# When the held output chunks run, and which buffers the last batch's loads and outputs use

## The chip, the cores and the metric

The kernel runs on one core of one Trainium2 chip. A core has a matmul engine (TensorE, PE in the profile), which writes into PSUM banks; two engines that read those banks, VectorE (DVE) and ScalarE (ACT); GpSimd (POOL); and SyncE (SP), which here issues nearly all DMA transfers, one after another in the order of its queue. The metric is the device time of one execution in microseconds.

## The reference, cut to what matters

```
scores = (z @ z.T) / S                    # S = 3136, per batch, 8 batches
x      = u * (relu(scores)**2 @ v)        # D = 256
x1, x2, x3 = split(x @ w_proj)            # three times D columns
conv   = irfft(rfft(x2) * rfft(filter))   # along the sequence, length S
out    = (x1 * conv * x3) @ w_out
```

The attention part is by far the largest. The transform of length 3136 = 64 x 49 is done by matmuls with two small matrices, in two steps on the way in and two on the way out; between the steps the data go through DRAM, since the second step needs them in another order.

## The kernel before, in words

A batch is cut along the sequence into seven chunks (`CHUNKS`: 512, 384, 512, 384, 512, 384, 448 rows). For each chunk the attention product is accumulated in PSUM and multiplied by `u` (L1559). Then `add_proj` makes the gate x1 * x3 of the chunk (matmuls L897 and L909, product on DVE L917), and x2 of the chunk, on which the first transform step runs (L940, L755); the result is put into a DRAM scratch (`spec`, L762).

Behind the last chunk of a batch, `add_spectrum` works on 16 columns of the spectrum in eight groups of two. For each group in the last batch: `load_spec` brings the columns from DRAM (L787), `forward` is the second transform step (matmuls L808 and L816), DVE or ACT copies the PSUM bank out (L363 on DVE, L359 on ACT), two DVE products with the filter follow (L1012, `mul`), then the inverse step (matmuls L808, `inverse2`), a copy out by ACT or DVE into a tile of pool `gs` or `A`, and a store to a second scratch (L1062). The groups take their tiles in turn from the ring `xh` (even groups) and from pool `R` (odd groups).

`add_end` makes output chunks from the second scratch: a load (`load_c`, L799), the last transform step (matmuls L1101 and L1098, two halves of D), a product with the gate on DVE (L1104, tile `yT`), the matmul with `w_out` (L1132), a copy from PSUM into an output tile, and the store to `out` (L1160, two transfers for one chunk).

The order is set by a planner at build time (`Plan`): each piece is a task with an estimated cost, the tasks it depends on and the buffer slots it takes; the planner lays the tasks out on estimated times and so fixes, for good, the order of each engine's queue, SP's among them. PE tasks have kinds: `S` (scores), `W` (attention product), `FA`, `FB` and `FZ`, the last being taken when nothing else is ready. A task in SP's queue that has to wait holds up what stands behind it.

At the end of the program two things meet. The seventh batch (of eight) has only its chunks 0 to 2 finished in the usual place; its chunks 3 to 6 are held back (`HOLD = 3`), and are planned last, as `FZ` filler, with loads into `cut_in` (L799, they land early) and outputs in `outs`. The constant `then` names what their first matmul has to wait for: in the kernel before `q_`, the last square of the attention. The eighth batch's seven chunks are planned just before, in the order `FINAL = (0, 2, 4, 6, 1, 3, 5)`, loads into pool `A`, and outputs in `R_p` (two tiles) for even chunks and `xh_p` (three tiles) for odd ones. `load_spec` always takes tiles from `l_p`, of which there are two.

Of the kernel before, what the change touches and what calls it, by code (L numbers as in the profile page):

```python
# [11 lines left out]
P = 128  # L12
F32 = mybir.dt.float32
BF16 = mybir.dt.bfloat16
# [11 lines left out]
HOLD = 3  # L26
DELAY = 2
LATE_PUT, LATE_LOAD, LATE_TURN, LATE_C, LATE_D2 = 3.0, 1.0, 1.5, 2.5, 1.0
SPEC_LAG = 1
FINAL = (0, 2, 4, 6, 1, 3, 5)  # L30
# [3 lines left out]
ISSUED = "issued"  # L34
# [209 lines left out]
def kernel(  # L244
# [12 lines left out]
    B, S, D = u.shape  # L257
# [4 lines left out]
    NC = len(CHUNKS)  # L262
# [82 lines left out]
    def job(kind, emit, cost, deps=(), takes=(), **kw):  # L345
        if not isinstance(cost, dict):
            cost = {"PE": cost}
        return plan.add(Task(emit, cost, deps, takes, **kw), kind)
# [4 lines left out]
    def on(engine, emit, cost, deps=(), takes=(), **kw):  # L353
        return job(None, lambda e: emit(), {engine: cost}, deps, takes, **kw)
# [12 lines left out]
    def both(n, first="ACT"):  # L367
        a, d = c_act(n), c_dve(n)
        return {"ACT": a, "DVE": d} if first == "ACT" else {"DVE": d, "ACT": a}
# [409 lines left out]
    def by_row(d):  # L779
        return d[0:S, :].rearrange("(p x) d -> p x d", x=2 * NJ)  # L780

    def load_spec(src, j0, nj, deps, late=0.0):
        box = {}

        def go():
            box["t"] = l_p.tile()
            nc.sync.dma_start(out=box["t"][:KR, 0 : 2 * nj, :], in_=by_row(src)[:, ds(2 * j0, 2 * nj), :])  # L787

        t = on("SP", go, 0.45, [*deps, *((d, ISSUED) for d in loads[-1:])], [l_p.slots], moves=0.6 * nj, late=late)
        return in_order(t), box  # L790

    def load_c(src, c, deps, home):
# [88 lines left out]
    def add_proj(b, c, xt, xt_tasks):  # L881
# [83 lines left out]
            to_spectrum()  # L965
        return users, puts, gtasks

    def add_spectrum(b, puts):
        deps0 = list(h_done) + list(tz_done) if b == 0 else []
        final = b == B - 1  # L970
        per = 2 if final else 4
        lasts = []
        behind = []
        ldb, gb = [None], [None]
        for g in range(NJ // 2):
            own = not final or g % 2 == 0
            xh, gh = (xh_p, gs_p) if own else (R_p, A_p)
            if 2 * g % per == 0:
                ldb[0] = load_spec(D1[b % 2], 2 * g, per, puts, LATE_LOAD * (not final))
            ld, ibox = ldb[0]  # L980
            ends_load = (2 * g + 2) % per == 0
            xb = {}
            evs = []
            firsts = []
            for i in range(2):
                j = 2 * g + i
                box = {}

                def mm(i=i, j=j, box=box, xb=xb, ibox=ibox, xh=xh):
                    box["p"] = bank()  # L990
                    if i == 0:
                        xb["x"] = xh.tile([P, 2, 4, D], BF16)
                    x = ibox["t"][:KR, ds(2 * (j % per), 2), :].rearrange("p c d -> p (c d)")
                    forward(box["p"], x, j)

                def ev(e, i=i, box=box, xb=xb):
                    copy(e, xb["x"][:KC, 0, ds(2 * i, 2), :].rearrange("p c d -> p (c d)"), box["p"][:KC, :])

                a = pe("FB", mm, c_line(j), [ld, *deps0, *firsts], [ps_m.slots, *([] if i else [xh.slots])])
                firsts = [a]  # L1000
                if i == 0:
                    a0 = a
                elif ends_load:
                    a.frees.append((ld, 0))
                e_ = job(None, ev, both(2 * D), [a])
                e_.frees.append((a, 0))
                evs.append(e_)

            def mul(i, g=g, xb=xb):
                x = xb["x"][:KC].rearrange("p i (j c) d -> p i j c d", c=2)  # L1010
                h = H[:KC, ds(2 * g, 2), i].unsqueeze(2).to_broadcast([KC, 2, 2, D])
                nc.vector.tensor_tensor(x[:, 1 - i], x[:, 0], h, ALU.mult)  # L1012

            def add(xb=xb):
                x = xb["x"][:KC].rearrange("p i (j c) d -> p i c j d", c=2)
                nc.vector.tensor_tensor(x[:, 1, 0], x[:, 1, 0], x[:, 0, 1], ALU.subtract)
                nc.vector.tensor_tensor(x[:, 1, 1], x[:, 1, 1], x[:, 0, 0], ALU.add)

            cost = c_dve2(4 * D)
            w_ = on("DVE", lambda mul=mul: mul(0), cost, evs, prio=ZP)  # L1020
            w_ = on("DVE", lambda mul=mul: mul(1), cost, [w_], prio=ZP, lat=ZL)
            z_ = w_ if final else on("DVE", add, 2 * c_dve2(2 * D), [w_], prio=ZP)

            def inv(g=g, xb=xb, z_=z_, a0=a0, gh=gh):
                if 2 * g % per == 0:
                    gb[0] = {"es": [], "firsts": []}
                gx = gb[0]
                for i in range(2):
                    j = 2 * g + i
                    box = {}  # L1030
                    new = j % per == 0

                    def mm(j=j, box=box, new=new):
                        box["p"] = bank()
                        if new:
                            gx["g"] = gh.tile([P, 2 * per, D], BF16)
                        z, y = (xb["x"][:KC, i, ds(j % 2 * 2, 2), :].rearrange("p c d -> p (c d)") for i in range(2))
                        if final:
                            inverse2(box["p"], y, z, j)
                        else:  # L1040
                            inverse(box["p"], y, j)

                    def ev(e, j=j, box=box):
                        copy(e, gx["g"][:KR, ds(2 * (j % per), 2), :].rearrange("p c d -> p (c d)"), box["p"][:KR, :])

                    a = pe(
                        "FB", mm, c_line(j) * (1 + final), [z_, *gx["firsts"], *(minus_task if final else [])], [ps_m.slots] + ([gh.slots] if new else [])
                    )
                    gx["firsts"] = [a]
                    if new:  # L1050
                        gx["g0"] = a
                    if i:
                        a.frees.append((a0, 1))
                    e_ = job(None, ev, both(2 * D), [a])
                    e_.frees.append((a, 0))
                    gx["es"].append(e_)
                if (2 * g + 2) % per:
                    return
                j0 = 2 * g + 2 - per

                def put():
                    nc.sync.dma_start(  # L1062
                        out=by_row(D2[b % 2])[:, ds(2 * j0, 2 * per), :], in_=gx["g"][:KR, 0 : 2 * per, :]
                    )

                p_ = on("SP", put, 0.4, gx["es"], moves=0.5 * per, late=LATE_D2 * (not final))
                p_.frees.append((gx["g0"], 1))
                lasts.append(p_)

            behind.append(inv)  # L1070
            if g >= SPEC_LAG:
                behind.pop(0)()
        for x in behind:
            x()
        return lasts

    def add_end(b, lasts, gtasks, cs, kind="FB", src=c_p, dsts=(o_p,), late=0, behind=(), then=(), split=False):
        for c in cs:
            t0, nt = T0[c], len(tiles[c])
            w = CHUNKS[c]  # L1080
            dst = dsts[c % len(dsts)]
            ld, cb = load_c(D2[b % 2], c, lasts, src)
            yb = {}
            ys = []
# [392 lines left out]
    for gi, g in enumerate(groups):  # L1477
# [22 lines left out]
        for i, un in enumerate(g):  # L1500
# [43 lines left out]
            if last:  # L1544
# [24 lines left out]
                if c == NC - 1:  # L1569
                    mine = [x for x in x_evs if x[0] == b]  # L1570
                    gts = [t for x in mine for t in x[2]]
                    lasts = add_spectrum(b, [p for x in mine for p in x[1]])
                    if b < B - 2:
                        add_end(b, lasts, gts, range(NC))
                    elif b == B - 2:
                        add_end(b, lasts, gts, range(HOLD))
                        held = lasts, gts
                        held_w = w_
                    else:
                        add_end(b, lasts, gts, FINAL, "FB", A_p, (R_p, xh_p), split=True)  # L1580
                        early = [*held[0], held_w]
                        outs = (o_p, cut_out, cut_out, cut_out, o_p, o_p)
                        add_end(b - 1, early, held[1], range(HOLD, NC), "FZ", cut_in, outs, 4, [(loads[-1], ISSUED)], [q_])
                    if b == 0:
                        hold = Held(v_p.slots, v_slot[0])
                        w_.frees.append((hold, 0))
                    else:
                        w_.frees.append((cv[b][0], 0))
# [56 lines left out]
```

## Time and profile before

| | |
|---|---|
| median of three runs | 1046.08 us (1042.27 to 1046.51) |
| the profiled execution | 1042.6 us, of it a span of 1040.7 us |
| mean granted TensorE clock in it | 0.992 |
| PE busy | 989.8 us (95%) |
| ACT busy | 912.6 us (88%) |
| DVE busy | 819.1 us (79%) |

Times in the views below are microseconds from the span's start. A row of the chain of waits gives a start, a duration and what ran or was waited for. A row of a timeline gives a start, the time from there to the end of its last instruction, engine, line, operation, `out<-in`, and the count of instructions merged in it; instructions of one engine overlap a little, so that the distance of two starts is what one instruction costs its engine, and the duration is what its user waits for. A row of the stage table gives a stretch, its length, each engine's busy time with its count, the granted TensorE clock, the DMA engines' busy share and the GB/s they moved. `SPq` is SP issuing transfers. The KB of a transfer are units of 1024 bytes.

### The profile page before, as it was taken

The numbers are of one execution on the slowest core, as the hardware profiler recorded it, in microseconds if no ns is written. First come the engines' busy times: TensorE is split into PE (matmuls) and PEld (weight loads), VectorE is DVE, ScalarE is ACT, GpSimd is POOL, SyncE is SP. The second block draws the span as 40 slices with busy tenths as digits, with TensorE's granted clock in tenths as the row PEclk, the third lists the DMA queues.
The fourth block names the chain that finished last, engine by engine and source line by source line (L and its number), as shares of the span: only waits on it lengthen the run. The fifth ranks groups of instructions, "written<-read, shape, count | busy, mean of one in ns | idle before, by whom it ended". The sixth has DMA issues, their size and how long they took to land.

```text
span 1040.7 us, 17903 instructions
## 1 busy us (share of the span) xinstructions
PE 989.8 (95%) x6010; PEld 480.7 (46%) x6078; DVE 819.1 (79%) x1497; ACT 912.6 (88%) x1273; POOL 190.4 (18%) x401
## 2 busy tenths in 40 slices
PE   5999899999999999999999999999999999999974
PEld 2444444444444545445454454444544454444553
DVE  6867588977788768986879777997879968897673
ACT  6998799987999889997999889997989989999672
POOL 5033111311023300313021311121202230001000
PEclk9999999999999999999999999999999999999997
DMA  9599767888887868899888979798887977868357
GB/s 165 96 157 180 136 141 147 164 147 164 184 159 138 170 135 206 167 153 145 160 203 156 172 170 181 147 173 157 193 174 147 161 167 163 201 137 184 83 157 214
DMA packets 324380, 167.99 MB, mean 161 GB/s; under 512 B 234088, under 2 KB 302184, under 8 KB 324288
## 3 DMA queue, kind: packets, MB, share of 16 engines
q1 hardware_dynamic: 296560, 135.87, 59.7%
q0 software_dynamic: 27728, 30.97, 21.7%
q8 instruction: 48, 0.79, 0.3%
q14 instruction: 44, 0.36, 0.1%
HBM read 90.26 MB, written 53.35 MB: 138 GB/s over the span
## 4 chain that ended last, share of the span: by engine, by line
PE 75%; DVE 8%; ACT 7%; DMA 5%; issue 3%; SPq 1%; another core or an unknown queue 0%; ACTq 0%; DVEq 0%; POOL 0%; POOLq 0%
PE ps_o_t L1365 40%; PE ps_s_t L1335 11%; PE ps_m_t L940 4%; ACT R_t L1510 4%; PE ps_m_t L1132 4%; PE ps_m_t L909 3%; PE ps_m_t L897 3%; PE ps_m_t L755 2%; DMA M_t<-A_t 2%; PE ps_m_t L824 2%; PE ps_m_t L1101 2%; PE ps_m_t L816 2%; DVE xT_t L1559 2%; DVE A_t L1519 2%; ACT A_t L1517 1%
## 5 line engine op out<-in xcount | busy, mean ns | idle before, releaser
L1510 ACT ACTIVATE R_t<-ps_s_t 128x1024 f32<-128x1024 f32 (+2 forms) x552 | 485.0, 921 | 33.3 <-PE ps_s_t L1335 27.8
L1365 PE MATMUL ps_o_t<-A_t,v_t 128*128 128x512 bf16 (+2 forms) x2011 | 465.4, 354 | 3.6 <-issue 0.5
L1365 PEld LDWEIGHTS <-v_t 128*128 128x128 bf16 x2688 | 253.6, 98 | 241.6 <-issue 30.0
L1519 DVE TENSOR_TENSOR A_t<-R_t 128x768 bf16<-128x768 f32 (+2 forms) x271 | 290.7, 1080 | 35.2 <-ACT R_t L1510 29.4
L1517 ACT ACTIVATE A_t<-R_t 128x768 bf16<-128x768 f32 (+3 forms) x281 | 265.8, 958 | 5.4 <-DMA spec<-s_t 0.9
L1335 PE MATMUL ps_s_t<-zT_t 64*128 64x512 bf16 (+2 forms) x1088 | 155.3, 358 | 3.7 <-ACT R_t L1510 3.0
L408 POOL COPY tick<-xT_t 1x1 bf16<-1x1 bf16 x54 | 15.9, 294 | 737.5 <-DVE xT_t L1559 737.5
L1559 DVE SCALAR_TENSOR_TENSOR xT_t<-ps_o_t,uT_t 128x256 bf16<-128x256 f32 (+1 forms) x224 | 76.5, 383 | 29.1 <-PE ps_o_t L1365 18.4
L917 DVE TENSOR_TENSOR gate_t<-ps_m_t,x_t 128x256 bf16<-128x256 f32 (+1 forms) x208 | 69.0, 385 | 30.8 <-PE ps_m_t L909 15.1
L1365 PE MATMUL ps_o_t<-M_t,v_t 128*128 128x384 bf16 (+2 forms) x336 | 79.1, 346 | 6.7 <-DMA M_t<-A_t 6.6
L1012 DVE TENSOR_TENSOR xh<-xh,H 100x1024 bf16<-100x1024 bf16 x120 | 81.5, 684 | 2.3 <-ACT xh L359 1.4
L1335 PEld LDWEIGHTS <-zT_t 64*128 64x128 bf16 x1088 | 32.9, 94 | 101.8 <-issue 99.8
L359 ACT ACTIVATE x_t<-ps_m_t 128x512 bf16<-128x512 f32 (+3 forms) x114 | 61.7, 564 | 16.7 <-PE ps_m_t L897 12.2
L363 DVE CAST x_t<-ps_m_t 128x512 bf16<-128x512 f32 (+3 forms) x99 | 60.0, 621 | 15.6 <-PE ps_m_t L940 10.8
L1104 DVE TENSOR_TENSOR yT_t<-ps_m_t,gate_t 128x512 bf16<-128x512 f32 (+2 forms) x97 | 58.2, 619 | 16.3 <-PE ps_m_t L1101 12.5
L363 DVE CAST s_t<-ps_m_t 128x512 bf16<-128x512 f32 (+1 forms) x72 | 45.9, 644 | 25.9 <-PE ps_m_t L755 24.4
L399 POOL DMA_DIRECT2D un_t<-in_u_dram x112 | 60.0, 558 | 8.7 <-issue 6.5
L418 POOL DMA_DIRECT2D v_t<-in_v_dram x112 | 59.4, 555 | 4.6 <-issue 2.5
L940 PE MATMUL ps_m_t<-wp,xT_t 128*128 128x256 bf16 x396 | 57.6, 274 | 0.5 <-DVE gate_t L917 0.3
L1132 PE MATMUL ps_m_t<-wo,yT_t 128*128 128x256 bf16 (+1 forms) x348 | 54.9, 278 | 0.2
L897 PE MATMUL ps_m_t<-xT_t,wp 128*128 128x512 bf16 (+2 forms) x203 | 51.7, 353 | 2.0 <-DVE xT_t L1559 1.7
L1365 PE MATMUL ps_o_t<-M2e_t,v_t 128*128 128x512 bf16 (+1 forms) x192 | 51.7, 370 | 0.3 <-issue 0.2
(179 smaller groups left out, 961.7 us busy)
## 6 DMA issues: line engine op xcount, KB each, us to landing
out_dram<-ost_t SPq DMA_DIRECT2D x49, 256.0 KB
spec<-s_t SPq DMA_DIRECT2D x88, 128.0 KB
spec_in_t<-spec SPq DMA_DIRECT2D x28, 392.0 KB
spec<-gs_t SPq DMA_DIRECT2D x28, 392.0 KB
out_dram<-ost_t SPq DMA_DIRECT2D x47, 192.0 KB
v_t<-in_v_dram POOLq DMA_DIRECT2D x56, 128.0 KB, 4.3
un_t<-in_u_dram POOLq DMA_DIRECT2D x56, 128.0 KB, 5.1
conv_in_t<-spec SPq DMA_DIRECT2D x26, 256.0 KB
```

The lines of the kernel that those rows point to most:

```text
L363: nc.vector.tensor_copy(out_, in_)
L897: nc.tensor.matmul(box["p"][:, :cw], wp16[:, k, ds(nb * P, P)], xt["t"][:, k, :cw], start=(k == 0), stop=(k == 1),)
L917: nc.vector.tensor_tensor(g[:, ::-1] if h == 0 else g, p, x, ALU.mult)
L940: nc.tensor.matmul(box["p"][:, ds(k_ * D, D)], xt["t"][:, k, ds((at + k_) * P, P)], wp16[:, k, ds(D, D)], start=(k == 0), stop=(k == 1),)
L1012: nc.vector.tensor_tensor(x[:, 1 - i], x[:, 0], h, ALU.mult)
L1132: nc.tensor.matmul(box["p"][:rows, ds(i * D, D)], yb["y"][:, k, ds((i0 + i) * P, rows)], wo16[:, k, :], start=(k == 0), stop=(k == 1),)
L1335: nc.tensor.matmul(ps[:m, i, :cw], zt[h, ds(t * P, m)], zt[h, ds(C0[c], cw)], start=True, stop=True)
L1365: nc.tensor.matmul(o, row(v16[b], t)[:, ds(dh * P, P)], x, start=(k == 0 and i == 0), stop=(last and i == len(pair) - 1),)
L1510: nc.scalar.activation(box["R"][:rows, 0:n, :cw], live[un][:rows, 0:n, :cw], AF.Relu)
L1517: nc.scalar.activation(a, r, AF.Square)
L1519: nc.vector.tensor_tensor(a, r, r, ALU.mult)
L1559: nc.vector.scalar_tensor_tensor(x, f, inv_s2, ut, ALU.mult, ALU.mult)
```

## The change

Three edits, all at the end of the program.

- `then` of the held chunks becomes the last inverse matmul (`inverses[-1]`, being issued is enough). Their outputs go, by place in their order instead of by chunk number, to `cut_out`, `cut_out`, `cut_out`, `o_p`.
- In the last batch `load_spec` takes its tiles in turn from `l_p`, `c_p` and `un_p`, two tiles each.
- The last batch's output tiles are taken from `R_p, xh_p, gs_p, R_p, xh_p, gs_p, xh_p`, by place in the order.

```diff
-    def load_spec(src, j0, nj, deps, late=0.0):
+    def load_spec(src, j0, nj, deps, late=0.0, home=l_p):
...
-            box["t"] = l_p.tile()
+            box["t"] = home.tile([P, 8, D] if home is l_p else [P, 4, D], BF16)
...
-        t = on("SP", go, 0.45, [*deps, *((d, ISSUED) for d in loads[-1:])], [l_p.slots], moves=0.6 * nj, late=late)
+        t = on("SP", go, 0.45, [*deps, *((d, ISSUED) for d in loads[-1:])], [home.slots], moves=0.6 * nj, late=late)
...
+    inverses = []
...
-                ldb[0] = load_spec(D1[b % 2], 2 * g, per, puts, LATE_LOAD * (not final))
+                ldb[0] = load_spec(D1[b % 2], 2 * g, per, puts, LATE_LOAD * (not final), (l_p, c_p, un_p)[g % 3] if final else l_p)
...
+                    inverses.append(a)
...
-        for c in cs:
+        for at, c in enumerate(cs):
...
-            dst = dsts[c % len(dsts)]
+            dst = dsts[at % len(dsts)]
...
-                        add_end(b, lasts, gts, FINAL, "FB", A_p, (R_p, xh_p), split=True)
+                        add_end(b, lasts, gts, FINAL, "FB", A_p, (R_p, xh_p, gs_p, R_p, xh_p, gs_p, xh_p), split=True)
                         early = [*held[0], held_w]
-                        outs = (o_p, cut_out, cut_out, cut_out, o_p, o_p)
-                        add_end(b - 1, early, held[1], range(HOLD, NC), "FZ", cut_in, outs, 4, [(loads[-1], ISSUED)], [q_])
+                        outs = (cut_out, cut_out, cut_out, o_p)
+                        add_end(b - 1, early, held[1], range(HOLD, NC), "FZ", cut_in, outs, 4, [(loads[-1], ISSUED)], [(inverses[-1], ISSUED)])
```

## The prediction

> **What bounds the kernel now.** The order of instructions built for the changed kernel is the same as before on every engine up to the last spectrum, so only the end of the program can change. I read it first in the chain of waits in order of time:
>
> ```profile
> 986.70 2.50 DMA spec_in_t<-spec
> ...
> 1010.92 0.70 DVE R_t L1012
> ...
> 1012.24 1.09 ACT A_t L359 x2
> ...
> 1013.35 2.85 DMA spec<-A_t
> ...
> 1016.69 4.34 DMA A_t<-spec
> ```
>
> Three stretches: the last spectrum (989.2 to about 1012.5, DVE rows in the chain), a trip through DRAM (store, then load) in which no engine of the chain computes, and the last batch's outputs. The stage table, with the DMA's rate in the last column:
>
> ```profile
> 989.20:1012.50 23.30, 19.02 (x141) 13.65 (x142) 20.17 (x37) 16.44 (x32) 0.00 (x0) 1.00 0.47 144
> 1012.50:1019.60 7.10, 1.56 (x10) 0.65 (x7) 0.00 (x0) 1.95 (x5) 0.00 (x0) 0.53 0.87 246
> ```
>
> In the spectrum DVE is busy 20.17 of 23.3 us, the most of the three; in the gap it does nothing and PE 1.56 us, while the DMA engines are at 0.87. The third stretch is cut by what the DMA does:
>
> ```profile
> 1015.90:1023.70 7.80, 3.65 (x29) 2.95 (x29) 2.67 (x4) 0.69 (x2) 0.00 (x0) 0.53 0.98 261
> 1023.70:1025.30 1.60, 1.60 (x24) 1.43 (x22) 1.46 (x3) 1.45 (x3) 0.00 (x0) 1.00 0.17 46
> 1025.30:1029.20 3.90, 2.54 (x26) 2.01 (x25) 2.03 (x4) 1.21 (x3) 0.00 (x0) 1.00 0.92 264
> 1029.20:1030.40 1.20, 0.89 (x11) 0.67 (x10) 0.66 (x2) 0.62 (x3) 0.00 (x0) 1.00 0.05 17
> ...
> 1036.00:1038.00 2.00, 0.00 (x0) 0.00 (x0) 0.00 (x0) 0.00 (x0) 0.00 (x0) 0.71 0.89 295
> ...
> 1039.20:1040.70 1.50, 0.00 (x0) 0.00 (x0) 0.00 (x0) 0.00 (x0) 0.00 (x0) 0.50 0.00 0
> ```
>
> From 1015.9 to 1039.2 it moves at 261 to 295 GB/s but for two holes, of 1.60 and 1.20 us. The second hole is this wait of ACT, which has no third `R` tile to write to:
>
> ```profile
> 1028.24 1.08 ACT L359 ACTIVATE R_t<-ps_s_t 128x512 f32<-128x512 f32 x2 [2.69 <-DMA out_dram<-R_t]
> ```
>
> So three different things bound the end: DVE, then DRAM latency, then DMA volume with holes.
>
> **Part 1: the held outputs leave the spectrum.** Their eight gate products (`yT`, L1104), and whatever else DVE does in the spectrum:
>
> ```profile
> 989.20:1012.50 23.30, 4.13 (x8) 1.00 0.47 144
> ```
> ```profile
> 990.29 0.62 DVE L363 CAST x_t<-ps_s_t 128x448 bf16<-128x448 f32 x1 [0.43 <-PE ps_s_t L897]
> 990.84 0.68 DVE L363 CAST R_t<-ps_o_t 100x512 bf16<-100x512 f32 x1
> 991.43 0.68 DVE L1012 TENSOR_TENSOR xh<-xh,H 100x1024 bf16<-100x1024 bf16 x1
> 992.03 0.69 DVE L1012 TENSOR_TENSOR R_t<-R_t,H 100x1024 bf16<-100x1024 bf16 x1
> ...
> 993.84 0.68 DVE L917 TENSOR_TENSOR gate_t<-ps_m_t,x_t 128x256 bf16<-128x256 f32 x2
> 994.44 0.68 DVE L917 TENSOR_TENSOR gate_t<-ps_o_t,x_t 128x256 bf16<-128x256 f32 x2
> ...
> 998.62 0.68 DVE L363 COPY v_t<-ps_o_t 128x512 f32<-128x512 f32 x1
> ...
> 1007.14 1.42 DVE L1012 TENSOR_TENSOR xh<-xh,H 100x1024 bf16<-100x1024 bf16 x2 [0.59 <-ACT xh L359]
> 1009.40 0.69 DVE L363 CAST R_t<-ps_s_t 100x512 bf16<-100x512 f32 x1 [0.84 <-PE ps_s_t L816]
> 1010.20 1.42 DVE L1012 TENSOR_TENSOR R_t<-R_t,H 100x1024 bf16<-100x1024 bf16 x2
> ```
>
> Before, DVE takes from 990.29 to 1010.20 + 1.42 = 1011.62, 21.3 us. In the changed order its queue over the same work holds 16 filter products, a cast of 448 columns, five casts of 512 and two pairs of gate products; the eight `yT` and the `v_t` copy come behind the last filter product. A product costs 0.60 us from start to start (991.43 to 992.03), as do a cast and a gate pair, and the first cast 0.55. The sum is 16 x 0.60 + 0.55 + 5 x 0.60 + 2 x 0.60 = 14.35 us. It also stands so that no two products of one group follow each other (those pairs take 1.42 instead of 1.29). That is 7.0 us less at best. ACT has the remaining 27 of 32 copies in that stage. One costs it 0.49 us (998.53 to 999.01 in the rows of part 3; two in the chain take 1.09), 27 x 0.49 = 13.2 us, just under DVE, so some waits remain. The rows show two of 0.59 and 0.84 us; I keep 0.6 us and take a gain of 6.4 us. Ends: 4.7 us (only the products and the 0.60 us copy come back, all waits stay) and 7.0 us.
>
> **Part 2: loads into three pools.** The 0.84 us wait hangs on a forward matmul that was late for want of a load tile. With six tiles SP issues six loads without waiting for a group to be done, so no price is left on the path. What speaks against it is that the first load, on the path with 2.50 us, shares the engines with five others; the first of seven `A_t` loads below takes 3.4 us. That is up to 0.9 us, for a transfer of 256 instead of 196 KB and behind stores; I take 0 (the six are issued after it) and leave 0.9 us to the range.
>
> **Part 3: what the gap hides, and SP's queue.** The last inverse matmul is at T:
>
> ```profile
> 1012.04 0.27 PE L808 MATMUL ps_o_t<-R_t,TZ 100*98 100x256 bf16 x1
> ...
> 1019.63 1.03 PE L1101 MATMUL ps_s_t<-T,A_t 128*128 128x128 bf16 x8 [5.57 <-DMA A_t<-spec]
> ```
> ```profile
> 1013.35 0.31 SPq L1062 DMA_DIRECT2D spec<-A_t  x1
> 1014.77 1.11 SPq L1160 DMA_DIRECT2D out_dram<-ost_t  x2
> 1016.25 4.12 SPq L799 DMA_DIRECT2D A_t<-spec  x7
> 1024.23 7.96 SPq L1160 DMA_DIRECT2D out_dram<-R_t  x8
> 1032.30 5.73 SPq L1160 DMA_DIRECT2D out_dram<-xh  x8
> ```
>
> T = 1012.04, the last store lands at T + 4.16 (1013.35 + 2.85), the loads are issued from T + 4.21, and the outputs start at T + 7.6. The held work now falls between T and T + 7.6: eight products, 4.1 us of DVE, and as much of PE and ACT; it fits. But SP's new order has the first held chunk's two stores ahead of the seven loads, and the other six held stores behind these. What a chunk's steps cost:
>
> ```profile
> 997.76 0.60 PE L1132 MATMUL ps_s_t<-wo,yT_t 128*128 128x256 bf16 x4
> ```
> ```profile
> 998.53 0.61 ACT L359 ACTIVATE ost_t<-ps_s_t 128x512 f32<-128x512 f32 x1
> 999.01 0.41 ACT L359 ACTIVATE v_t<-ps_o_t 128x256 f32<-128x256 f32 x1
> ```
>
> From T the first chunk needs the four inverse matmuls (0.5, estimated from 0.27 for one and 0.60 for four of L1132), its first step of L1101 (0.3, estimated from 1.03 for eight at half clock), two products (2 x 4.13 / 8 = 1.05), a matmul group (0.6) and ACT's two copies (0.48 + 0.41 = 0.9): T + 3.35. The upper bound is the 4.6 us from the first output matmul (1019.63) to its store (1024.23) now: T + 5.1. Its two stores take SP 1.11 us, so the loads start at T + 4.46, 0.25 us later than now. Whatever delays these two stores delays everything after them.
>
> **Part 4: the DMA's volume behind T.** Sizes:
>
> ```profile
> out_dram<-ost_t SPq DMA_DIRECT2D x3, 256.0 KB
> A_t<-spec SPq DMA_DIRECT2D x4, 256.0 KB
> out_dram<-ost_t SPq DMA_DIRECT2D x3, 192.0 KB
> A_t<-spec SPq DMA_DIRECT2D x3, 192.0 KB
> out_dram<-v_t SPq DMA_DIRECT2D x2, 192.0 KB
> ```
>
> The held chunks store 1728 KB in all; before, 1280 KB of them were gone before 1014.77. Now all come after T: 384 KB ahead of the loads (1600 KB), 1344 KB behind them, then the outputs' 3136 KB. That is 6.62 MB, against 5.31 MB now. The holes go: the held stores fill the first, and seven output tiles for seven chunks the second. The stream began at 1015.9, 1.1 us after the stores at 1014.77, so it will begin at T + 3.35 + 1.1 = T + 4.45. The first 2.03 MB (two stores, seven loads) go at the 261 GB/s of that mix: 7.8 us. The other 4.59 MB are stores alone; their rows lie between 264 and 295 GB/s. With up to eight in flight I take the middle, 280: 16.4 us. SP issues faster than that (0.58 us for some 200 KB), so the DMA sets the end. With 1.5 us behind the last byte the end is T + 4.45 + 7.8 + 16.4 + 1.5 = T + 30.15, against T + 28.66 now: the tail grows by 1.5 us.
>
> The fastest row here is the 295 GB/s, and the row of 261 had the DMA engines busy 0.98 of the time. [...]
>
> **The sum.** 6.4 - 1.5 = 4.9 us, a span of 1035.8 and a profiled execution of 1037.7 us against 1042.6. That execution stands 3.5 us under the median of the runs shown, and two of the three runs lie near 1046, one near 1042. I put the change on the middle of these runs, 1044.4: 1039.5 us.
>
> **The rivals.**
> - The DMA keeps pace with SP. In a full queue the stores then go at 320 GB/s, beyond any row above: 4.59 MB take 14.3 us, and the gain is 7.0 us, with the full part 1 7.6 us: 1037. For it: the row at 295 had a share of only 0.89. Against: the row of 261 had 0.98. [...]
> - The spectrum stays bound by its waits. Gain of 4.7 us there, stores at 264: 17.4 us, the tail grows by 2.5; gain 2.2 us: 1042. For it: ACT's 13.2 us stand so near DVE's 14.35 that the two may wait for each other in turn, now that no held work fills in.
> - Slower: the two held stores ahead of the loads in SP's queue. If they come late, all seven loads and everything behind wait. Each us costs one; it decides from 4.9 us (stores at T + 8.3) on, and by 10 us late (an output product held up by a buffer that the spectrum or an earlier load still has) it is 1049.5, slower by 0.5%. For it: the seven loads are the only thing the end needs, and they now stand behind a chain over PE, DVE, PE and ACT. Against: each step of that chain is first in its queue behind the spectrum.
>
> That the change does nothing is excluded: the built order has all held matmuls behind the last inverse.
>
> **How the numbers follow.** A measurement of this kernel can tell about 0.5%, 5.2 us, from no change. The forecast (gain 3.5 to 6.5 us) has 0.58; it lies on both sides of that bound, and since the full queue speaks for rates above the middle I split it 0.30 faster, 0.28 same. The fast stores have 0.18, faster; the waiting spectrum 0.14, same; the late stores 0.10, slower. Faster 0.48, same 0.42, slower 0.10. The range leaves out the late stores and the outermost of the others: from the fast stores on the lower runs (1042.3 - 7.6 = 1034.7, rounded to 1034) to the waiting spectrum on the upper ones with the late first load (1046.5 - 2.2 + 0.9 = 1045).
>
> **What would show it.** Part 1: last filter product about 1004.6 instead of 1010.9, no L1104 on DVE before it. Part 2: six loads issued back to back. Part 3: PE, DVE and ACT busy in the gap; loads issued within 0.5 us of the last store's landing. Part 4: no hole in the DMA's rate from the loads to the end, no wait of ACT for a store, and about 30 us from T to the end. The forecast is wrong if the spectrum takes over 18 us, if the loads wait for the held stores, or if the rate in the tail lies under 250 or over 300 GB/s.

## The result and the profile after

The changed kernel takes 1036.74 us (median of 8 runs, 1034.06 to 1041.28) against 1044.05 us for the kernel before beside it (8 runs, 1042.06 to 1046.51). The ratio is 0.993, with a 95% interval of 0.9908 to 0.9953: faster by 0.5 to 0.9%. The profiled execution has a span of 1033.2 us against 1040.7. Line numbers of the changed file are two higher than before behind L967 and three higher behind L1055: L1014 is the filter product (L1012 before), L1065 the spectrum's store, L1104 and L1135 the output matmuls, L1107 the gate product, L1163 the output store.

The chain of waits after, in order of time (start, duration, what):

```profile
984.95 2.81 DMA spec_in_t<-spec
...
1002.71 0.61 DVE R_t L1014
...
1006.11 0.88 ACT v_t L359 x2
...
1008.36 3.44 DMA A_t<-spec
...
1023.40 0.60 ACT xh L359
```

The first load of the spectrum is issued at 984.95 instead of 986.70. Up to there both kernels run the same instructions in the same order, so this 1.75 of the 7.5 us is variation between executions; the kernel before, profiled a second time (run e12), issued it at 988.67. I therefore count from this issue. From it to the end of the last spectrum matmul (1004.28 after, 1012.63 before) it was 25.9 us and is 19.3; from there to the end it was 28.1 and is 28.9. The sum is 5.75 us.

DVE's timeline after (start, time to the end of the last one, instruction, count, idle time before it):

```profile
988.86 0.62 DVE L363 CAST x_t<-ps_s_t 128x448 bf16<-128x448 f32 x1 [1.21 <-PE ps_s_t L897]
...
990.60 0.69 DVE L1014 TENSOR_TENSOR R_t<-R_t,H 100x1024 bf16<-100x1024 bf16 x1
991.20 0.69 DVE L1014 TENSOR_TENSOR xh<-xh,H 100x1024 bf16<-100x1024 bf16 x1
...
1002.63 0.68 DVE L1014 TENSOR_TENSOR R_t<-R_t,H 100x1024 bf16<-100x1024 bf16 x1
1004.49 0.56 DVE L1107 TENSOR_TENSOR yT_t<-ps_s_t,gate_t 128x384 bf16<-128x384 f32 x1 [1.19 <-PE ps_s_t L1104]
```

No held product stands in the spectrum any more, and DVE runs without a pause from 988.86 to 1003.31, 14.45 us. SP's timeline shows all eight loads gone by 990.2, and the two held stores ahead of the loads of the last batch:

```profile
984.95 0.34 SPq L787 DMA_DIRECT2D spec_in_t<-spec  x1
...
989.88 0.31 SPq L787 DMA_DIRECT2D conv_in_t<-spec  x1
994.50 0.31 SPq L1065 DMA_DIRECT2D spec<-gs_t  x1
...
1007.01 1.14 SPq L1163 DMA_DIRECT2D out_dram<-v_t  x2
1008.36 3.85 SPq L799 DMA_DIRECT2D A_t<-spec  x7
1012.31 3.82 SPq L1163 DMA_DIRECT2D out_dram<-v_t  x4
```

The stage table behind the spectrum (columns as in the table before; the last three are granted clock, DMA share, GB/s) has no hole any more from the loads' issue on:

```profile
1004.30:1008.36 4.06, 3.64 (x42) 2.79 (x40) 3.50 (x7) 2.59 (x6) 0.00 (x0) 1.00 0.47 148
1008.36:1011.80 3.44, 1.81 (x17) 0.99 (x14) 1.00 (x2) 2.22 (x6) 0.00 (x0) 1.00 0.95 253
1011.80:1014.80 3.00, 2.79 (x21) 1.99 (x22) 1.89 (x3) 0.23 (x1) 0.00 (x0) 0.55 1.04 288
1014.80:1017.60 2.80, 2.76 (x29) 2.22 (x27) 2.33 (x4) 2.10 (x4) 0.00 (x0) 0.87 1.09 364
1017.60:1020.60 3.00, 2.99 (x33) 2.22 (x31) 2.28 (x5) 2.38 (x6) 0.00 (x0) 1.00 0.91 297
1020.60:1023.60 3.00, 2.50 (x25) 1.61 (x22) 1.86 (x4) 2.04 (x6) 0.00 (x0) 1.00 0.84 291
1023.60:1026.60 3.00, 0.00 (x0) 0.00 (x0) 0.00 (x0) 0.68 (x2) 0.00 (x0) 0.86 0.90 252
1026.60:1030.50 3.90, 0.00 (x0) 0.00 (x0) 0.00 (x0) 0.00 (x0) 0.00 (x0) 0.50 0.87 286
```

From 1011.8 to 1030.5 it moves 295 GB/s in the mean (the rows weighted by their lengths).

### The profile page after: what moved, and what is told of

It is laid out like the page before. It is cut to its first block, busy times and chain, and to the rows that moved or that the text cites. A ratio compares the mean times of both kernels' runs of the same rounds, so it can differ in the third digit from the quotient of the medians.

```text
span 1033.2 us, 17968 instructions
## 1 busy us (share of the span) xinstructions
PE 993.5 (96%) x6078; PEld 480.8 (47%) x6078; DVE 817.7 (79%) x1496; ACT 914.0 (88%) x1274; POOL 190.8 (18%) x401
## 4 chain that ended last, share of the span: by engine, by line
PE 76%; DVE 7%; ACT 7%; DMA 5%; issue 3%; SPq 2%; ACTq 0%; DVEq 0%; POOL 0%; POOLq 0%
PE ps_o_t L1368 40%; PE ps_s_t L1338 11%; PE ps_m_t L940 4%; PE ps_m_t L1135 4%; PE ps_m_t L909 4%; ACT R_t L1513 3%; PE ps_m_t L897 3%; DMA M_t<-A_t 3%; PE ps_m_t L755 2%; PE ps_m_t L1104 2%; PE ps_m_t L824 2%; PE ps_m_t L816 2%; DVE xT_t L1562 2%; DVE xh L1014 1%; ACT A_t L1520 1%
## 5 line engine op out<-in xcount | busy, mean ns | idle before, releaser
L1513 ACT ACTIVATE R_t<-ps_s_t 128x1024 f32<-128x1024 f32 (+2 forms) x552 | 485.4, 922 | 28.6 <-PE ps_s_t L1338 23.7
L1368 PE MATMUL ps_o_t<-A_t,v_t 128*128 128x512 bf16 (+2 forms) x2064 | 474.8, 355 | 0.7 <-ACT A_t L1520 0.3
L1522 DVE TENSOR_TENSOR A_t<-R_t 128x768 bf16<-128x768 f32 (+2 forms) x271 | 290.9, 1080 | 35.6 <-ACT R_t L1513 29.5
L1014 DVE TENSOR_TENSOR xh<-xh,H 100x1024 bf16<-100x1024 bf16 x120 | 81.5, 685 | 1.6 <-ACT xh L359 0.8
L1107 DVE TENSOR_TENSOR yT_t<-ps_m_t,gate_t 128x512 bf16<-128x512 f32 (+2 forms) x97 | 58.3, 620 | 21.2 <-PE ps_m_t L1104 17.0
L1135 PE MATMUL ps_m_t<-wo,yT_t 128*128 128x256 bf16 (+1 forms) x348 | 55.2, 277 | 0.7 <-DVE yT_t L1107 0.5
L359 ACT ACTIVATE xh<-ps_m_t 100x512 bf16<-100x512 f32 (+1 forms) x84 | 50.5, 629 | 3.7 <-PE ps_m_t L808 2.1
```

The source lines that it names most:

```text
L359: nc.scalar.activation(out_, in_, AF.Copy)
L1135: nc.tensor.matmul(box["p"][:rows, ds(i * D, D)], yb["y"][:, k, ds((i0 + i) * P, rows)], wo16[:, k, :], start=(k == 0), stop=(k == 1),)
L1368: nc.tensor.matmul(o, row(v16[b], t)[:, ds(dh * P, P)], x, start=(k == 0 and i == 0), stop=(last and i == len(pair) - 1),)
L1513: nc.scalar.activation(box["R"][:rows, 0:n, :cw], live[un][:rows, 0:n, :cw], AF.Relu)
L1522: nc.vector.tensor_tensor(a, r, r, ALU.mult)
```

## The experiments

Two theories were put against each other. Theory A is that of the prediction: DVE's queue sets the length of the last spectrum, so what counts is that the held work leaves it, and the loads' pools matter little. Theory B: late loads set it, and the held work only fills DVE's waits. Each run gives a ratio to the kernel before, timed beside it, and the profile of one execution. From the profiles, in us:

| run | ratio (95%) | first load's issue to last spectrum matmul | to the issue of the last batch's loads | from there to the end |
|---|---|---|---|---|
| before | | 25.9 | 29.6 | 24.5 |
| e12, before again | 0.9998 (0.9978 to 1.0018) | 26.2 | 30.0 | 24.8 |
| whole change | 0.993 (0.9908 to 0.9953) | 19.3 | 23.4 | 24.8 |
| e1, `then` alone | 1.0001 (0.9984 to 1.0018) | 29.1 | 33.2 | 26.1 |
| e2, loads alone | 0.9977 (0.9956 to 0.9997) | 22.1 | 27.7 | 26.1 |
| e3, output tiles alone | 0.9982 (0.9963 to 1.0002) | 29.1 | 33.0 | 23.8 |
| e4, all but `then` | 0.9945 (0.9922 to 0.9969) | 22.1 | 27.8 | 24.2 |
| e5, all but the loads | 1.0015 (1.0001 to 1.003) | 28.1 | 32.8 | 24.3 |
| e6, all but the tiles | 0.9949 (0.9928 to 0.9971) | 19.4 | 23.6 | 26.1 |
| e7, three held chunks not stored | 0.9924 (0.9895 to 0.9952) | 19.4 | 23.5 | 23.6 |
| e8, two chunks held instead of four | 0.9948 (0.9928 to 0.9968) | 19.2 | 24.6 | 24.5 |
| e9, four load tiles | 0.9904 (0.9887 to 0.9922) | 20.5 | 24.5 | 23.9 |
| e10, e5 and extra matmuls | 1.0011 (0.9995 to 1.0028) | 28.9 | 33.0 | 24.1 |
| e11, stores on two queues | 0.9943 (0.9915 to 0.9972) | 19.2 | 23.3 | 26.7 |

The expectations count the spectrum from the first load's landing to the start of the last inverse group: 22.85 us before, 3.1 less than the column here; in the other runs the difference lies between 3.2 and 4.0 us, since their first load takes up to 0.4 us longer (2.94 us in e10 against 2.50) and the last group is slower at a fallen clock (four inverse matmuls took 0.85 us in e1 at 0.50, 0.44 in e10 at 1.00). The tail in them runs from that group to the end. The same tail differs by up to 0.9 us between executions (24.8 in the whole change, 23.9 in e9, with the same work), so smaller differences in the last column say nothing.

### One edit alone

e1, against the kernel before (the other two edits left out):

```diff
-                        outs = (o_p, cut_out, cut_out, cut_out, o_p, o_p)
+                        outs = (cut_out, cut_out, cut_out, o_p)
...
-                        ... [(loads[-1], ISSUED)], [q_])
+                        ... [(loads[-1], ISSUED)], [(inverses[-1], ISSUED)])
```

> Only the held outputs wait for the last inverse matmul; two load tiles, output tiles from R and xh as before. Theory A (DVE's queue sets the spectrum): from the first load's landing to the last inverse 17.5 to 18.5 us instead of 22.85 (the 4.7 us of held DVE work gone, the waits on late loads stay), the tail from there to the end 31 to 32.5 us instead of 28.66 (more DMA volume, and the wait of ACT for a third R tile stays): 1 to 3 us faster than before. Theory B (late loads set the spectrum, the held work rides in DVE's waits): 21.5 us or more for the spectrum, and slower than before by 1 us or more.

Neither more nor less than nothing: 1.0001. The spectrum of the profiled execution is 29.1 us, about 25 by the expectation's count: theory A's 17.5 to 18.5 is far off, and B's "21.5 or more" holds, though not its "slower by 1 us or more". SP's timeline of e1:

```profile
987.65 5.30 SPq L787 DMA_DIRECT2D spec_in_t<-spec  x4
997.30 0.31 SPq L1065 DMA_DIRECT2D spec<-gs_t  x1
997.70 0.34 SPq L787 DMA_DIRECT2D spec_in_t<-spec  x1
998.13 0.36 SPq L1065 DMA_DIRECT2D spec<-A_t  x1
998.58 0.34 SPq L787 DMA_DIRECT2D spec_in_t<-spec  x1
1003.58 0.31 SPq L1065 DMA_DIRECT2D spec<-gs_t  x1
1004.65 0.31 SPq L787 DMA_DIRECT2D spec_in_t<-spec  x1
```
```profile
SPq L1065 <- DVE gs_t L363: 4.3, 1, 4.3
```

With two tiles the planner has placed only four loads ahead of the first store of the spectrum. The fifth stands behind that store, for which SP waits 4.3 us (second fence, the waits of SP: who waits for whom, us in total, times, longest). Before the change five stand ahead. The store is not what holds the fifth load, though: its tile serves the third group until about 997.4 (that group's last forward matmul starts at 996.99), and the load goes out at 997.70. Nor does PE, whose matmuls alone read the loads, wait for one behind the first, here or in e5. The two tiles act through the order that the planner fixed for PE. The fifth group's first forward matmul stands in e1 behind the inverse matmuls of four groups, in the changed kernel behind those of two; the first row is e1's, the second that of the changed kernel:

```profile
1003.56 0.63 PE L816 MATMUL ps_s_t<-spec_in_t,S 98*100 98x512 bf16 x1
```
```profile
994.04 0.38 PE L816 MATMUL ps_o_t<-conv_in_t,S 98*100 98x512 bf16 x1
```

That is 15.9 us behind the first load's issue (15.4 in e5) instead of 9.1. Until then PE, DVE and ACT wait for each other over the few groups that are loaded: from 997.80 to 1000.33 PE runs one matmul. The granted clock, the third figure from the end of a row, falls in the stage table of e1:

```profile
993.00:998.00 5.00, 3.74 (x26) 2.69 (x24) 4.91 (x11) 2.95 (x7) 0.00 (x0) 1.00 0.23 73
998.00:1003.00 5.00, 2.98 (x14) 2.72 (x15) 2.88 (x5) 1.73 (x4) 0.00 (x0) 0.66 0.51 161
1003.00:1008.00 5.00, 4.02 (x15) 2.51 (x14) 3.27 (x5) 2.82 (x6) 0.00 (x0) 0.50 0.48 141
```

e2, against the kernel before: only the edit of `load_spec` and its call.

> Only the loads of the last spectrum use three pools. Theory A: DVE's queue still holds 20 us of work, so the spectrum takes 21 to 22.5 us instead of 22.85 and the tail 28.7 as before: 0.4 to 1.8 us faster. Theory B: the spectrum falls to 18 us or less, 4 us or more faster.

The kernel is 0.23% faster (0.03 to 0.44%), 2.4 us, between the two theories, and so is the spectrum: 18.7 us by the expectation's count. The loads alone are worth 3.9 us there, in which the held work still stands. A part of this is given back behind it, where held stores left over stand in SP's queue: from the last spectrum matmul to the loads it takes 5.6 us (27.7 - 22.1) instead of 3.6.

e3, against the kernel before:

```diff
-                        add_end(b, lasts, gts, FINAL, "FB", A_p, (R_p, xh_p), split=True)
+                        add_end(b, lasts, gts, FINAL, "FB", A_p, (R_p, xh_p, gs_p, R_p, xh_p, gs_p, xh_p), split=True)
```

with the index by place in the order.

> Only the output tiles are taken from R, xh and gs in turn. Theory A: the spectrum stays at 22.8 us, the hole of 1.2 us in the DMA's rate and ACT's wait for a store go, the tail is 26 to 27.5 us instead of 28.66: 1.2 to 2.6 us faster. Rival: the stores are bound by the DMA's rate anyway, the tail stays over 28.2 us.

The ratio of 0.9982 does not tell this from no change. The tail behind the loads is 0.7 to 1.0 us shorter than in the two profiles of before, hardly more than it differs between executions. The spectrum, whose order is that of before, took 29.1 us in this execution instead of 25.9, and for its last 7 us the clock had fallen, as the stage table of e3 shows.

```profile
1005.60:1010.60 5.00, 3.48 (x25) 2.61 (x24) 4.69 (x8) 4.45 (x10) 0.00 (x0) 1.00 0.41 121
1010.60:1015.00 4.40, 3.04 (x16) 2.10 (x17) 1.38 (x2) 2.54 (x5) 0.00 (x0) 0.75 0.90 264
1015.00:1019.40 4.40, 3.32 (x14) 2.36 (x13) 2.08 (x3) 1.79 (x3) 0.00 (x0) 0.50 0.67 219
```

The fall came behind a wait of PE for the seventh load, 4.9 us after its issue at 1006.10; before, the same load had landed within 3.1 us and PE did not wait. When PE goes on, 2.2 of the 3.2 us are already lost, at a clock still of 1.00:

```profile
1011.02 0.63 PE L816 MATMUL ps_s_t<-spec_in_t,S 98*100 98x512 bf16 x2 [1.70 <-DMA spec_in_t<-spec]
```

e12 is there to tell whether that belongs to the tiles; it is the kernel before, unchanged.

> The kernel before once more, for a second profile of the same order of work. The run with the output tiles alone had the same order in the spectrum as before, and took 29.1 us there at a granted clock that fell to 0.5 in its last 9 us, against 25.9 us at 1.0. If the clock falls in some executions and not in others, this profile shows either 25.9 us with the clock at 1.0, or about 29 us with a fallen clock, and the ratio is 1.000 within 0.003. If the output tiles made the difference, it shows 25.9 us and 1.0.

Its spectrum took 26.2 us at a clock of 1.00, so two profiles of before have no fallen clock there and e3 has one. The times speak for chance: the profiled execution of e3 is the longest of its ten (1048.81 us, median 1044.57) and has the lowest mean granted clock of them (0.985, the others 0.987 to 0.991), and the kernel before, timed beside it, spreads in the same way, from 1040.06 us at 0.992 to 1050.73 at 0.984. That does not show where in the program its clock fell, so it is not settled. The ratio of e12, 0.9998, shows what equal kernels give.

### One edit undone

e4, against the changed kernel (`outs` in the order that gives each held chunk its old tile):

```diff
-                        outs = (cut_out, cut_out, cut_out, o_p)
+                        outs = (cut_out, o_p, o_p, o_p)
...
-                        ... [(inverses[-1], ISSUED)])
+                        ... [q_])
```

> Loads and output tiles changed, the held outputs start when the last square is done, as before. Theory A: the sum of the two, spectrum 21 to 22.5 us, tail 26 to 27.5 us: 2 to 4 us faster than before and slower than the whole change by 3 to 5 us. Theory B: the spectrum falls to 18 us or less and the kernel is as fast as the whole change or faster, because the DMA volume behind the spectrum is smaller.

0.9945, 5.7 us faster than before, more than theory A allowed. By the profiles the wait of the held outputs, on top of the loads and tiles, takes 4.4 us from the way to the loads (27.8 to 23.4) and gives 0.6 back behind them. By the ratios it is worth 0.15%, 1.6 us, with intervals that overlap; so the times do not show that moving the held work adds anything to the other two edits (e6 against e2, 0.28%, points the same way, with intervals that overlap too).

e5, against the changed kernel:

```diff
-(l_p, c_p, un_p)[g % 3] if final else l_p
+l_p
```

> The whole change but for the loads, which keep their two tiles. Theory A: with the held work gone DVE needs 14.4 us for eight groups, 1.8 us a group, and each pair of load tiles has to turn over in 3.6 us with 2.8 us of it for a transfer; the spectrum takes 16.5 to 18.5 us instead of the 15.9 of the whole change, the tail is the same 29.5 us: 0.6 to 2.6 us slower than the whole change. Rival: the loads are in time with two tiles, under 0.4 us.

This is the run that decides: 1.0015, not faster than before at all. Expected was 0.6 to 2.6 us lost against the whole change; it is 8.9 us by the ratios (1.0015 - 0.993, of 1045) and the spectrum is 8.8 us longer in the profiles. SP's and PE's order are as in e1, and the clock has fallen here too, to 0.50 from 1007.6 to the end of the spectrum.

e6, against the changed kernel: output tiles `(R_p, R_p, R_p, R_p, xh_p, xh_p, xh_p)` by place, which is the old assignment.

> The whole change but for the output tiles: even chunks in two R tiles, odd ones in xh. Theory A: with the DMA queue full the third even chunk waits longer for the store of the first, since the held stores stand ahead of it; a hole of 1 to 3 us, tail 30.5 to 32.5 us instead of 29.5. Rival: held stores in the queue cover the wait, and the tail stays at 29.5 to 30.

0.9949, 2 us less gain than the whole by the ratios, with intervals that overlap; 1.3 us in the tail behind the loads. e2 against e4 gives 1.9 us, e1 against e5 1.8 us, all in the same direction. So in the tails of the profiles the tiles are worth 1 to 2 us. The times do not show it: e5, with the tiles, is not faster than e1 without them (1.0015 against 1.0001).

### What sets the tail

e7, against the changed kernel, leaves the held chunks 4 to 6 unstored (that part of the output is missing):

```diff
             def store(i0, n, c=c, ob=ob):
+                if b == B - 2 and c >= HOLD + 1:
+                    return
```

> The whole change, but the held chunks 4 to 6 are computed and not stored (that part of the output is left out): 1344 KB less behind the loads. If the DMA's volume sets the end (theory A), the tail is shorter by 3.8 to 5 us (1.38 MB at 280 to 360 GB/s): about 25 us instead of 29.5. If SP's issue of stores or the outputs' computing sets it, by 1.5 us or less.

1.38 MB less shorten the tail behind the loads by 1.3 us only (by 0.3 against e9, which has the same stores as the whole change), where the volume alone, at the expectation's 280 to 360 GB/s, would have given 3.8 to 5 (the whole change moved 295 in the mean and 364 in its fastest row). The stage table of e7 shows what comes in its place:

```profile
1014.00:1017.00 3.00, 2.29 (x19) 1.56 (x20) 1.89 (x3) 0.00 (x0) 0.00 (x0) 0.67 1.15 308
1017.00:1020.00 3.00, 3.00 (x29) 2.48 (x27) 2.04 (x4) 2.04 (x4) 0.00 (x0) 0.76 0.33 80
1020.00:1023.00 3.00, 2.95 (x31) 2.17 (x31) 2.29 (x5) 2.39 (x5) 0.00 (x0) 1.00 0.96 262
```

A hole at 80 GB/s, while PE is busy all the time: no output is ready yet (SP waits 4.1 us for ACT's first `R` tile). In the changed kernel the held stores lie in that hole, and so cost little.

e8, against the changed kernel, is `HOLD = 5` instead of 3.

> The whole change, but only chunks 5 and 6 of the seventh batch are held (HOLD = 5): 896 KB of stores leave the tail and two chunks' outputs go into the attention of the last batch, where PE is busy 99%. Theory A: the tail is shorter by 2.5 to 3.3 us (29.5 to about 26.5), the attention longer by two chunks of PE work, 2 x 1.6 us = 3.2 us (estimated from 16 to 24 matmuls of 0.06 to 0.11 us each a chunk): within 1 us of the whole change. If PE has room there, 2 us faster than the whole change.

0.9948, and no shorter tail (24.5 us): it gains nothing. e7 leads one to expect this, since the volume that it moves away was nearly free. Besides, the loads go out 1.2 us later than in the whole change, because four held stores stand ahead of them instead of two.

e11, against the changed kernel:

```diff
-                    nc.sync.dma_start(
+                    eng = nc.gpsimd if b == B - 1 and j else nc.sync
+                    eng.dma_start(
```

> The whole change, and the second of the two stores of each output chunk of the last batch is issued by GpSimd, which is idle there, instead of by SP. If SP's pace of issuing (0.6 us a store, and stores that wait in line) holds the end, the tail from the last spectrum matmul to the end is 1.5 to 4 us shorter than 28.9 us. If the DMA's rate holds it, it stays within 1 us, or grows because GpSimd's transfers start later.

The tail is not shorter but 1.9 us longer behind the loads. GpSimd has issued its last store by 1029.2 of 1037.9, SP by 1030.5. The last rows of the timelines of GpSimd and SP:

```profile
1028.17 1.04 POOL L1164 DMA_DIRECT2D out_dram<-xh  x2 [0.47 <-ACT xh L359]
```
```profile
1028.07 2.44 SPq L1164 DMA_DIRECT2D out_dram<-xh  x2
```

From the loads' issue to the end of the last store's issue it is 19.3 us; with all stores on SP it was 21.2 to 22.2 (whole change, e5, e9 and e10, whose tails have the same stores). So two queues have the stores issued 1.9 to 2.9 us sooner, and the end comes no sooner. What makes e11 longer comes behind the last issue: 7.4 us to the end, against 2.6 to 2.7 in every other run. What the program waits for there stays open.

### How many loads, and what the clock costs

e9, against the changed kernel: `(l_p, c_p)[g % 2]`, four tiles.

> The whole change, but the loads take four tiles (two of the pool before, two of one more) in turn instead of six. SP's queue again has all eight loads ahead of the first store of the spectrum, as with six. If what counts is that no load stands behind a store of the spectrum, the spectrum (first load's issue to the end of its last matmul) is that of the whole change, 19.3 us, within 0.7. If the number of loads in flight counts, 21 us or more.

The spectrum takes 20.5 us, 1.1 more than with six tiles and so a little outside the 0.7, but far from the 28 of two. All eight loads again stand ahead of the first store, and the fifth group's forward matmuls start 9.2 us behind the first load. The ratio of 0.9904 (0.9887 to 0.9922) is at least as good as that of the whole change; the intervals overlap, so it is not shown to be faster.

The 1.1 us do not belong to the number of loads. PE runs the same matmuls as in the whole change, and for 13.2 us from its first forward matmul on it starts them within 0.03 us of the same times (the first matmul itself starts 0.12 us later behind the load's issue). The rest of the difference comes behind that, with a granted clock that fell here (0.70 from 1002 to 1004, 0.50 from 1004 to 1006) and not in the whole change (1.00), after the same wait of PE for DVE. The row of the whole change, that of e9, and the last row of e9's stage table of the spectrum:

```profile
1000.96 0.27 PE L808 MATMUL ps_m_t<-R_t,zT_t 100*98 100x256 bf16 x1 [0.89 <-DVE R_t L1014]
```
```profile
1002.68 0.29 PE L808 MATMUL ps_m_t<-R_t,zT_t 100*98 100x256 bf16 x1 [0.89 <-DVE R_t L1014]
```
```profile
996.06:1005.56 9.50, 8.35 (x48) 6.35 (x47) 8.97 (x17) 7.56 (x15) 0.00 (x0) 0.85 0.34 106
```

So four tiles do what six do.

e10, against e5: two extra matmuls of 512 columns in front of each inverse group.

```diff
                         if final:
+                            for _ in range(2):
+                                nc.tensor.matmul(box["p"][:KR, :], TZ[:KC, 3, 0:KR], H[:KC, 0].rearrange("p c d -> p (c d)"), start=True, stop=True)
                             inverse2(box["p"], y, z, j)
```

> As the run without the loads' change (two load tiles), and two further matmuls of 512 columns ahead of each of the 16 inverse groups, whose result is overwritten: PE work that waits for no DVE result. If the halved TensorE clock is what makes that spectrum long (28.1 us against 25.9 before the change), the granted clock stays at 1.0 there and the spectrum is 24 to 26 us, though PE has 32 x 0.22 = 7 us more to do. If late loads alone make it long, it stays at 28 us or grows, whatever the clock.

The clock stays at 1.00 through the spectrum, and it still takes 28.9 us. Rows of its stage table, and of its chain of waits, where L1042 is the extra work:

```profile
1000.00:1005.00 5.00, 3.17 (x21) 2.09 (x20) 3.83 (x7) 1.94 (x4) 0.00 (x0) 1.00 0.54 161
1005.00:1010.00 5.00, 3.72 (x23) 2.37 (x22) 2.48 (x4) 3.25 (x6) 0.00 (x0) 1.00 0.41 111
```
```profile
997.67 0.43 PE ps_o_t L1042 x2
...
1017.69 0.43 PE ps_m_t L1042 x2
```

Twelve such pairs lie on the chain, 5.2 us. Without them it would be 23.7 us (an estimate that takes the chain to shorten by just that), against 28.1 at the fallen clock and 19.3 with six tiles. So by this estimate the order that goes with two tiles costs something like 4.4 us and the clock as much again; the run by itself does not part them, since the extra work took the clock's gain away.

## Why the prediction was right, and where it was not

The direction and the size were right: forecast 1039.5 us in a range of 1034 to 1045, measured 1036.74; forecast a gain of 4.9 us, measured 7.3 by the medians and 5.75 from the first load on. The 5.75 us lie in the forecast's own case (3.5 to 6.5). The 7.3 us lie beyond it, where the rival of the fast stores was, but they are not its doing: the stores did not reach its 320 GB/s in the mean, and 4.9 to 9.6 us are within the interval of the ratio. The reasons of the forecast were right only in part.

**Part 1** counted 14.35 us of DVE work; DVE ran 14.45 us without a pause. From the first load's landing to the last inverse group it was 22.84 us and is 15.92, 6.9 us less, where 6.4 were taken and 7.0 was the upper end.

**Part 2 is the step that failed.** "With six tiles SP issues six loads without waiting for a group to be done, so no price is left on the path", and the whole 6.4 us were put to part 1. That no price was left came true; that the loads have no share in the gain did not. The runs show that part 1 without part 2 is worth nothing (e1 1.0001, e5 1.0015) and that part 2 by itself takes 3.9 us from the spectrum (e2). With part 2 in place, part 1 takes another 2.8 us (e4 against the whole change, in the profiles; the times alone do not show it). The sum came out because both edits are in the change, and its DVE count holds only where the loads are early. That was luck: the same reasoning expected 1 to 3 us from `then` alone. The error was to price each edit against the kernel before, where the held work covered the late loads: I named DVE's wait of 0.84 us as all that the loads cost, and did not ask what would show once the cover was gone. The rival of a spectrum "bound by its waits" had its waits between ACT and DVE, not in the loads. The 0.9 us that six loads in flight might cost the first one came to 0.3 (2.81 instead of 2.50).

**Part 3** was right to 0.2 us: held stores at T + 3.33 (forecast 3.35), loads from T + 4.68 (4.46), with T = 1003.68. The held work fits between, and the two stores did not come late; the slower rival has no ground.

**Part 4**: from T to the end 29.5 us, forecast 30.15. The rate was 295 GB/s in the mean, with 364 in one stretch of 2.8 us and no more than 297 in the others; the rival with 320 was too high for the whole. The 280 of the forecast was taken between rows of 264 and 295, but the rows that it left out between them are slower:

```profile
1030.40:1034.00 3.60, 2.03 (x18) 1.36 (x17) 1.45 (x3) 3.02 (x9) 0.00 (x0) 1.00 0.91 242
1034.00:1036.00 2.00, 0.00 (x0) 0.00 (x0) 0.00 (x0) 0.00 (x0) 0.00 (x0) 1.00 0.80 255
```

From 1030.4 to 1039.2 the kernel before moves 248 GB/s in the mean. At that rate the 4.59 MB would have taken 18.5 us and the gain would have been 2.8 us, so it is luck too that the middle of 280 came out close. But "so the DMA sets the end" was only half true: e7 took 1.38 MB away and gained 1.3 us, where 4.9 follow at 280 GB/s. The other half is the computing of the outputs, which I had left out of the sum: without the held stores the DMA falls to 80 GB/s while PE is busy (e7). The holes went as said; ACT's wait of 2.69 us for a third `R` tile is gone (one of 0.30 us for a `gs` tile is left), and the tail of e6 puts 1.3 us on that edit.

## What to carry to other kernels

When several edits go together, price each one in the schedule that the others leave, not in the old one: work that looks like a burden may be covering a latency, and taking it away helps only if the latency goes too. Where the order of the queues is fixed at build time, a tile too few need not show as a wait for a load: it shows as work that stands late in another engine's queue. Here two more tiles (e9) brought the fifth group's forward matmuls from 15.4 us behind the first load to 9.2, which was worth more than the 4.1 us of work that the change moved. And before a volume of transfers is put at its full price, look for the hole it will lie in.

## What the runs showed that was not expected

TensorE's granted clock fell inside the program, in some executions and not in others, in stretches where PE waited. In e1 it went from 1.00 to 0.50 with PE busy 2.98 of 5 us in the stretch where it fell. In e3 it fell (0.75 with PE busy 3.04 of 4.4 us, then 0.50) in a spectrum that had the order of the kernel before, in whose two profiles it stayed at 1.00, one of them with PE busy 3.13 of 6 us near its end, as this row of e12's stage table shows:

```profile
1008.00:1014.00 6.00, 3.13 (x21) 2.09 (x20) 4.12 (x6) 4.00 (x8) 0.00 (x0) 1.00 0.78 226
```

The spectrum of e3 took 3.2 us longer than that of before, 2.2 of them ahead of the fall. The clearest pair is the whole change and e9: the same matmuls at the same times, the same wait of 0.89 us, and then a clock of 1.00 in the whole change and of 0.50 in e9. Why it fell in the one and not in the other, no run here shows. So the same instructions do not fix the time of these last 55 us. All seven profiles with six load tiles have the clock at 1.00 through the spectrum, but since e9 runs the same matmuls, that is not shown to be the tiles' doing.
